# Routed attention with a bilinear FFN on one core: when the softmax denominators are summed, and how the last key tile reaches the sum

## The chip, the core and the metric

The kernel runs on one core of a Trainium2 chip. The core has a matrix engine (TensorE, PE; its weight loads are PEld), a vector engine (VectorE, DVE), an activation engine (ScalarE, ACT), a general one (GpSimd, POOL) and one that only issues transfers (SyncE, SP). Each engine works through its own list of instructions in order, and semaphores make one engine wait for another. The kernel fixes all these lists itself, when it is built. The metric is the device time of one execution in microseconds, the median of several.

## What is computed

The reference, cut to what matters:

```python
# q, k, v: (4 batch, 8 heads, 768 tokens, 64); 16 cluster centroids per head
q_assign = argmax(normalized q @ normalized centroids)     # same for k
mask = q_assign[..., :, None] == k_assign[..., None, :]
scores = where(mask, q @ k.T / sqrt(64), -1e9)
attn = exp(scores - max(scores))
attn = attn / (attn.sum(-1) + 1e-9)
x = (attn @ v) as a (3072 tokens, 512) matrix
out = ((x @ w_a) * (x @ w_b)) @ w_out                      # w_a, w_b: 512 x 1536, w_out: 1536 x 512
```

Everything is float32. A row of attention is divided by its denominator, the sum of its exponentials over all 768 keys.

## The kernel before

The heads are taken in pairs, 16 in all: pair p belongs to batch element p // 4. For each pair the queries are cut into two halves of 384 tokens, and the keys into six tiles of 128. A unit u is one pair, one half and one key tile; it has 12 units per pair. The main loop takes two units per pass, called a group g; three groups make a half, six make a pair, and 96 groups make the attention. What stands in a group:

```python
for g in range(NG + 3):                  # NG = 96
    p, l = divmod(g, GPP)                # pair, and group within it (GPP = 6)
    now, before = (2*g, 2*g + 1), (2*g - 2, 2*g - 1)
    ...
    if 0 < g < NG:  score(now)           # TensorE: mask and q.k; ACT: exponentials pt
    check_inverses()
    if 0 < g <= NG:
        for u in before: add_up(u)       # sums of pt over the key tiles
    if 1 < g <= NG: weigh(before)        # TensorE: pt times v into O
    late = int(g > EARLY)
    if g % 3 == late and 0 < g - late:
        denominators(*divmod(g // 3 - 1, 2))
    if g < NG: ready[l]()                # prepares the next pair: transposes, clusters, one-hot
    ...                                  # due[g]: which weight parts are rounded in this group
    round_next()
    first, second = (4, 1) if g <= EARLY else (5, 3 if g < NG else 2)
    ph = {first: (p, 0), second: (p - 1, 1)}.get(l)
    halved = ph in den_of
    if halved: todo.extend(normalize(*ph))
    if ffn:                              # pieces of the FFN fill the rest of the group
        credit += PER_GROUP[...]
        while len(ffn) > least and credit > 0:
            cost, piece = ffn.popleft(); credit -= cost
            piece()
            if todo: todo.popleft()()
            round_next()
    else: credit = 0
    round_next()
    while todo: todo.popleft()()
    if halved: ffn_ready(*ph)            # FFN pieces of a batch element, once its x is whole
```

While the first batch element's attention runs (pairs 0 to 3, groups 0 to 23) there is no FFN to fill the groups; the FFN of a batch element runs beside the attention of the next.

The exponentials of one half are summed over the six key tiles (j from 0 to 5) in a tile acc of 128 x 768. In the first batch element (p < HP, HP = 4) VectorE adds; later the sum is made by accumulating transfers that POOL issues. Matmuls with ones then sum over the 128 keys of a tile:

```python
def add_up(u):
    p, hf, j = where(u)
    if j == 0 or j == NJ - 1 and p < HP: return
    if j == 1: accs[p, hf] = accp.tile([P, 2, HB], FP32, name="acc")
    acc = accs[p, hf]
    if p < HP:
        nc.vector.tensor_tensor(out=acc, in0=probs[u - 1] if j == 1 else acc, in1=probs[u], op=ALU.add)
        return
    if j == 1: nc.vector.tensor_tensor(out=acc, in0=probs[u - 1], in1=probs[u], op=ALU.add)
    else:      nc.gpsimd.dma_start(out=acc, in_=probs[u], accum_op=ALU.add)

def denominators(p, hf):
    ps = apart()
    acc = accs.pop((p, hf))
    terms = [acc]
    if p < HP: terms.insert(0, probs[p * UPP + hf * NJ + NJ - 1])    # the last key tile
    for n, t in enumerate(terms):
        for a in range(2):
            nc.tensor.matmul(out=ps[a * D:(a + 1) * D, 0:HB], lhsT=ones, rhs=t[:, a, :],
                             start=(n == 0), stop=(n == len(terms) - 1))
    nc.scalar.activation(out=acc[:, 0, :], in_=ps[:, 0:HB], func=AF.Copy, accum_out=...)
```

Normalization of a half takes three steps on VectorE (transpose, reciprocal, transpose back, on acc) and a multiply of x on POOL. Weights are rounded in 36 parts of 128 x 512: four instructions on VectorE and an add on POOL for each, then see_w checks their size with two activations on ACT and starts the next load:

```python
def round_w(i):     # vector: tensor_scalar, scalar_tensor_tensor (w); tensor_scalar, scalar_tensor_tensor (rest)
    ...             # gpsimd: w = w + rest
    unseen.append((i, upper half of raw))

def see_w():
    while unseen:
        i, upper = unseen.pop()
        nc.scalar.activation(out=size, in_=upper, func=AF.Abs)
        nc.scalar.activation(out=size, in_=size, func=AF.Relu, ..., accum_out=stat[:, n:n + 1])
        load_w(i + 2)
```

The up part of the FFN computes 2 x 2 blocks by seven products, p1 to p7, on sums and differences of blocks; T1 to T4 are the combinations of x, made on VectorE. The pieces come in the order p1, p2, p6, p5, p7, p3, p4; p6 reads T2, p7 reads T3. For the first batch element T2 is made when its x is whole, and T3 beside p2:

```python
elif n == 0:                       # first batch element
    ps[1] = both(ps[1], lambda: combine_x(b, "T3"))
    ps[3] = both(lambda: combine_x(b, "T4"), ps[3])
```

Of the kernel before, what the change touches and what calls it, by code (L numbers as in the profile page):

```python
# [8 lines left out]
FP32 = mybir.dt.float32  # L9
BF16 = mybir.dt.bfloat16  # L10
INT32 = mybir.dt.int32
UINT32 = mybir.dt.uint32
# [22 lines left out]
P = 128  # L35
# [107 lines left out]
def short_path(nc, tc, ctx, c, cn, centroids_in, casts, n_far, q, k, v,  # L143
# [126 lines left out]
        raws[i] = raw  # L270

    def round_w(i):
        w = w_parts[i][0]
        wi = w.bitcast(INT32)
        raw = raws.pop(i)
        halves = lambda dt: raw.bitcast(dt).rearrange("p (n two) -> p n two", two=2)
        lo, hi = halves(UINT32)[:, :, 0], halves(INT32)[:, :, 1]


        nc.vector.tensor_scalar(out=wi, in0=hi, scalar1=3, scalar2=0x3FFFFFF8,  # L280
                                op0=ALU.logical_shift_left,
                                op1=ALU.bitwise_and)
        nc.vector.scalar_tensor_tensor(out=wi, in0=hi, scalar=SIGN_TOP, in1=wi,
                                       op0=ALU.bitwise_and, op1=ALU.bitwise_or)

        rest = wtp.tile([P, WN], FP32, name="rest")
        nc.vector.tensor_scalar(out=rest.bitcast(INT32), in0=wi,
                                scalar1=SIGN_EXP, scalar2=None,
                                op0=ALU.bitwise_and)
        nc.vector.scalar_tensor_tensor(out=rest, in0=lo, scalar=2.0 ** -52,  # L290
                                       in1=rest, op0=ALU.mult, op1=ALU.mult)
        nc.gpsimd.tensor_tensor(out=w, in0=w, in1=rest, op=ALU.add)
        unseen.append((i, halves(FP32)[:, :, 1]))

    unseen = []

    def see_w():

        while unseen:
            i, upper = unseen.pop()
            size = spare()[0].bitcast(BF16)[:, 3 * WN:4 * WN]
            nc.scalar.activation(out=size, in_=upper, func=AF.Abs)
            n = 4 * NPAIR + i
            nc.scalar.activation(out=size, in_=size, func=AF.Relu, scale=-STEEP,
                                 bias=edge[:, 0:1], accum_out=stat[:, n:n + 1])
            load_w(i + 2)

    NSTAT = 4 * NPAIR + len(w_parts)  # L310
    edge = zero.tile([P, 1], FP32, name="edge")
# [231 lines left out]

    probs, accs, O_of, den_of, xTs = {}, {}, {}, {}, {}
    unchecked = []
    todo = deque()
    UPP = 2 * NJ
    NU = NPAIR * UPP
# [33 lines left out]

    def add_up(u):
        p, hf, j = where(u)
        if j == 0 or j == NJ - 1 and p < HP:
            return
        if j == 1:
            accs[p, hf] = accp.tile([P, 2, HB], FP32, name="acc")
        acc = accs[p, hf]
        if p < HP:  # L590
            nc.vector.tensor_tensor(out=acc, in0=probs[u - 1] if j == 1 else acc,  # L591
                                    in1=probs[u], op=ALU.add)
            return
        if j == 1:
            nc.vector.tensor_tensor(out=acc, in0=probs[u - 1], in1=probs[u],  # L595
                                    op=ALU.add)
        else:
            nc.gpsimd.dma_start(out=acc, in_=probs[u], accum_op=ALU.add)  # L598

    def weigh(us):  # L600
        for u in us:
# [16 lines left out]

    def denominators(p, hf):


        ps = apart()
        acc = accs.pop((p, hf))
        terms = [acc]
        if p < HP:
            terms.insert(0, probs[p * UPP + hf * NJ + NJ - 1])
        for n, t in enumerate(terms):
            for a in range(2):
                nc.tensor.matmul(out=ps[a * D:(a + 1) * D, 0:HB], lhsT=ones,  # L629
                                 rhs=t[:, a, :], start=(n == 0),  # L630
                                 stop=(n == len(terms) - 1))
# [149 lines left out]
    def ffn_ups(b, h):  # L781
# [109 lines left out]
        for n, (combinations, ps) in enumerate(parts):  # L891
            if n == 0 and b:
                ps[0] = both(*combinations, ps[0])
                ps[2] = both(lambda: combine_x(b, "T4"), ps[2])
            elif n == 0:
                ps[1] = both(ps[1], lambda: combine_x(b, "T3"))
                ps[3] = both(lambda: combine_x(b, "T4"), ps[3])
            if n + 1 < len(parts):
                for i, step in enumerate(parts[n + 1][0], 4):
                    ps[i] = both(ps[i], step)  # L900
            pieces += [(2 * HB, f) for f in ps]
# [10 lines left out]
    def ffn_downs(b, h):  # L912
# [96 lines left out]

        def before():  # L1010
            see_w()
            assert not raws
# [17 lines left out]
    def both(*fs):  # L1030
        return lambda: [f() for f in fs]
# [19 lines left out]
    def ffn_ready(p, hf):  # L1051

        b, hp = divmod(p, HP)
        if hp < HP - 1 or hf == 0:
            return
        if b > 0:
            h = []

            ffn.insert(len(ffn) - FREE_ROOM, (0, lambda: (
                up_room(b), combine_x(b, "T3"), combine_x(b, "T1"))))  # L1060
            ffn.insert(len(ffn) - 1, (0, lambda: combine_x(b, "T2")))
            ffn.extend(ffn_ups(b, h)[1])
        else:
            h = h_first
            combine_x(0, "T2")
            ffn.extend(ups_first + plain_ups(0, h, range(NF - 4, NF)))
        ffn.extend(ffn_downs(b, lambda: h))

# [18 lines left out]
    early = early_steps()  # L1087

    for _ in range(12):
        nc.tensor.matmul(out=idle[0:D, 0:D], lhsT=ones, rhs=ones, start=True,  # L1090
# [31 lines left out]
    for g in range(NG + 3):  # L1122
        p, l = divmod(g, GPP)
        if l == 0:
            ready = prep_steps(p + 1)
        now = (2 * g, 2 * g + 1)
        before = (2 * g - 2, 2 * g - 1)
        if g == 1:
            weigh(before)
        if 0 < g < NG:  # L1130
            score(now)
        check_inverses()
        if 0 < g <= NG:
# [9 lines left out]
        parts = due.get(g, [])  # L1143
        if g in early:
            todo.append(early[g])

        def round_next():
            if parts or not ffn:
                see_w()
            if parts:  # L1150
                i = parts.pop(0)
                round_w(i)
# [298 lines left out]
```

## Time and profile before

| what | value |
|---|---|
| time, median of 3 | 1055.83 us (1055.52 to 1056.8) |
| span of the profiled execution | 1052.8 us |
| TensorE busy | 1023.8 us, 97% |
| VectorE busy | 579.2 us, 55% |
| ScalarE busy | 336.5 us, 32% |
| GpSimd busy | 254.1 us, 24% |
| accumulating transfers acc<-pt | 96, of 384 KB each |

The profile is one execution. A line of a timeline has the start and the length in us, the engine, the line of the kernel, the operation, what it writes and reads by the program's names, and in brackets the idle time before it with what ended it. A line of waits has the waiting instruction, what it waited for, the total in us, how often, and the longest. The lines of the kernel that matter: L563 are the scores, L572 the exponentials, L591 and L595 the adds of VectorE into acc, L598 the accumulating transfers, L606 the product with v, L629 the denominators, L649 to L661 the normalization, L692 all FFN matmuls, L779 the combinations of x, L280 to L292 the rounding, L304 and L306 the size check. TensorE splits a float32 matmul in two, so a matmul of the program is two in the trace.

### The profile page before, as it was taken

How to read it: one execution, taken by the hardware profiler on the slowest of the kernel's cores; microseconds unless marked ns; L12 is line 12 of the kernel's file. 1: busy time of each engine (PE TensorE's matmuls, PEld its weight loads, DVE VectorE, ACT ScalarE, POOL GpSimd, SP SyncE). 2: the span in 40 equal slices, each digit the busy share in tenths (PEclk: the TensorE clock that was granted, in tenths of full speed). 3: DMA queues.
4: the chain of work that ended last, by engine and by line, in shares of the span. 5: the costliest groups of instructions: out<-in, count | busy, mean ns of one | idle time of the engine just before them, and what ended most of it. 6: DMA issues, size and time to landing. Idle time of an engine off the chain costs nothing.

```text
span 1052.8 us, 17688 instructions
## 1 busy us (share of the span) xinstructions
PE 1023.8 (97%) x7094; PEld 499.5 (47%) x7094; DVE 579.2 (55%) x1098; ACT 336.5 (32%) x674; POOL 254.1 (24%) x251
## 2 busy tenths in 40 slices
PE   8999989989999999999999999999999999999997
PEld 5443333334445554444444655444444566444564
DVE  6668777786658345443545535444443635444552
ACT  5666544444542213333233121233232201111100
POOL 1112234354332112222324211232222110212100
PEclk9999989999999999999999999999999999999999
DMA  7334546857574463626243372533322320000000
GB/s 181 87 83 88 102 90 147 167 129 154 140 156 86 94 112 65 109 46 106 54 81 65 78 134 54 91 61 66 60 45 50 76 56 21 1 1 1 6 31 29
DMA packets 134346, 84.24 MB, mean 80 GB/s; under 512 B 108144, under 2 KB 117360, under 8 KB 134256
## 3 DMA queue, kind: packets, MB, share of 16 engines
q0 software_dynamic: 13824, 37.75, 19.8%
q1 hardware_dynamic: 120016, 44.85, 19.0%
q8 instruction: 58, 0.95, 0.4%
q10 hardware_dynamic: 416, 0.43, 0.1%
q14 instruction: 32, 0.26, 0.1%
HBM read 37.78 MB, written 6.29 MB: 42 GB/s over the span
## 4 chain that ended last, share of the span: by engine, by line
PE 80%; DMA 6%; DVE 6%; issue 4%; POOL 2%; ACT 2%; DVEq 0%; POOLq 0%; SPq 0%; ACTq 0%
PE m L692 54%; PE s L563 12%; PE O L606 10%; DMA acc<-pt 5%; PE s L629 1%; PE m L629 1%; PE s L378 1%; DVE acc L591 1%; ACT pt L572 1%; PE m L378 1%; POOL xT L661 0%; DVE acc L595 0%; POOL acc L598 0%; POOL h L840 0%; PE m L362 0%
## 5 line engine op out<-in xcount | busy, mean ns | idle before, releaser
L572 ACT ACTIVATE pt<-s 128x768 f32<-128x768 f32 x192 | 146.2, 808 | 191.1 <-PE s L563 142.6
L598 POOL DMA_DIRECT2D acc<-pt x96 | 82.8, 862 | 261.1 <-DMA acc<-pt 161.5
L606 PE MATMUL O<-pt,v 128*64 128x384 f32 x768 | 145.0, 499 | 0.0
L563 PE MATMUL s<-qkT 64*128 64x384 f32 x768 | 140.3, 484 | 0.0
L840 POOL TENSOR_TENSOR h<-h,ha 128x384 f32<-128x384 f32 x66 | 72.8, 1110 | 214.6 <-DVE ha L834 213.7
L834 DVE TENSOR_TENSOR ha<-ha,m 128x384 f32<-128x384 f32 x88 | 48.1, 549 | 126.7 <-PE m L692 100.9
L830 ACT COPY h<-m 128x384 f32<-128x384 f32 x88 | 42.2, 480 | 213.3 <-PE m L692 209.9
L834 DVE TENSOR_TENSOR h<-h,m 128x384 f32<-128x384 f32 x88 | 48.2, 547 | 100.9 <-PE m L692 73.5
L606 PEld LDWEIGHTS O<-pt,v 128*64 128x64 f32 x768 | 46.6, 136 | 85.8 <-issue 77.9
L692 PE MATMUL m<-wo_sb,h 128*64 128x256 f32 x768 | 86.7, 379 | 0.0
L692 PE MATMUL m<-xT,wa_sb 128*64 128x384 f32 x480 | 83.7, 487 | 2.7 <-DVE ha L834 2.5
L563 PEld LDWEIGHTS s<-qkT 64*128 64x128 f32 x768 | 71.0, 188 | 31.8 <-issue 0.9
L692 PE MATMUL m<-xT,wb_sb 128*64 128x384 f32 x480 | 83.1, 486 | 0.4 <-DVE h L834 0.4
L692 PE MATMUL m<-raw 128*64 128x384 f32 x432 | 78.9, 486 | 0.0
L692 PEld LDWEIGHTS m<-wo_sb,h 128*64 128x64 f32 x768 | 56.1, 137 | 29.1 <-issue 3.7
L661 POOL TENSOR_TENSOR xT<-xT,acc 128x384 f32<-128x384 f32 x32 | 35.2, 1099 | 133.4 <-DVE acc L656 84.1
L692 PE MATMUL m<-xT,h 128*64 128x256 f32 x576 | 64.6, 379 | 0.0
L692 PE MATMUL m<-xT,pair 128*64 128x384 f32 x352 | 64.5, 487 | 0.0
L830 ACT COPY ha<-m 128x384 f32<-128x384 f32 x66 | 31.6, 478 | 98.8 <-PE m L692 93.2
L692 PEld LDWEIGHTS m<-xT,wa_sb 128*64 128x64 f32 x480 | 34.9, 137 | 46.1 <-issue 33.2
L692 PEld LDWEIGHTS m<-xT,wb_sb 128*64 128x64 f32 x480 | 34.6, 137 | 43.5 <-issue 37.0
L692 PEld LDWEIGHTS m<-xT,h 128*64 128x64 f32 x576 | 42.1, 137 | 21.4 <-issue 1.6
(180 smaller groups left out, 1323.6 us busy)
## 6 DMA issues: line engine op xcount, KB each, us to landing
acc<-pt POOLq DMA_DIRECT2D x96, 384.0 KB, 4.0
raw<-in_moe_w_a_dram SPq DMA_DIRECT2D x12, 512.0 KB, 4.2
raw<-in_moe_w_b_dram SPq DMA_DIRECT2D x12, 512.0 KB, 3.7
raw<-in_moe_w_out_dram SPq DMA_DIRECT2D x12, 512.0 KB, 3.9
qk<-in_q_dram SPq DMA_DIRECT2D x48, 96.0 KB, 3.3
qk<-in_k_dram SPq DMA_DIRECT2D x48, 96.0 KB, 3.7
v<-in_v_dram SPq DMA_DIRECT2D x24, 192.0 KB, 3.9
out_dram<-rest SPq DMA_DIRECT2D x24, 128.0 KB, 1.7
```

Of the source, the lines that this page charges most:

```text
L378: nc.tensor.matmul(out=ps[32 * kq:32 * kq + 32, 0:HB], lhsT=cTb[:, hp, :], rhs=qkTs[p][:, kq * HB:(kq + 1) * HB], start=True, stop=True)
L563: nc.tensor.matmul(out=s[:, a, 0:HB], lhsT=Ts[p][r, S + j * P:S + (j + 1) * P], rhs=Ts[p][r, hf * HB:(hf + 1) * HB], start=start, stop=not ...
L572: nc.scalar.activation(out=pt, in_=s[:, :, 0:HB], func=AF.Exp, scale=SCALE)
L591: nc.vector.tensor_tensor(out=acc, in0=probs[u - 1] if j == 1 else acc, in1=probs[u], op=ALU.add)
L598: nc.gpsimd.dma_start(out=acc, in_=probs[u], accum_op=ALU.add)
L606: nc.tensor.matmul(out=O_of[0][a * D:(a + 1) * D, 0:HB], lhsT=vs[p][:, a, j, :], rhs=probs[u][:, a, :], start=(j == 0), stop=(j == NJ - 1))
L629: nc.tensor.matmul(out=ps[a * D:(a + 1) * D, 0:HB], lhsT=ones, rhs=t[:, a, :], start=(n == 0), stop=(n == len(terms) - 1))
L661: nc.gpsimd.tensor_tensor(out=x, in0=x, in1=den, op=ALU.mult)
L692: nc.tensor.matmul(out=ps[half], lhsT=lhsT[:, half], rhs=rhs, **kw)
L830: nc.scalar.copy(out=box[name], in_=box["X"][:, 0:HB])
L834: nc.vector.tensor_tensor(out=box[name], in0=box[name], in1=box[bank][:, 0:HB], op=ALU.add)
L840: nc.gpsimd.tensor_tensor(out=to, in0=to, in1=box[name], op=ALU.mult)
```

## The change

The last key tile of the first batch element's halves (j = 5) is no longer a term of its own in the denominators, but is added to acc by an accumulating transfer, so that the denominators have one term everywhere. To leave time for it, the denominators of a half come a group later in the first batch element, and with them the normalization and the start of the FFN. In the later batch elements the transfers of odd key tiles (3 and 5) are issued at the end of their group, so that two in a row don't hold up POOL's list, and the denominators come after two FFN pieces of their group instead of ahead of them. Rounding and the size check of a weight part are cut into two steps each and are spread over the FFN pieces, T3 is made right after T2, and the rates of FFN and rounding are set to the later start.

The diff, cut (marked ...):

```diff
     def round_w(i):
...
+        def first():
+            see_w()
+            ...                          # the two vector instructions that write w
+        def second():
+            ...                          # the two that write rest, and the add on gpsimd
+            unseen.extend(see_steps(i))
+        return [first, second]
+
+    unseen = deque()
+    def see_steps(i):
+        def first():
+            ...
+            nc.scalar.activation(out=size, in_=upper[:, :, 1], func=AF.Abs)
+        def second():
+            nc.scalar.activation(out=size, in_=size, func=AF.Relu, ...)
+            del raws[i]
             load_w(i + 2)
+        return [first, second]
+
+    def see_w(steps=None):
+        for _ in range(len(unseen) if steps is None else min(steps, len(unseen))):
+            unseen.popleft()()
...
     def add_up(u):
         p, hf, j = where(u)
-        if j == 0 or j == NJ - 1 and p < HP:
+        if j == 0:
             return
...
-        if p < HP:
+        if p < HP and j < NJ - 1:
             nc.vector.tensor_tensor(out=acc, in0=probs[u - 1] if j == 1 else acc,
                                     in1=probs[u], op=ALU.add)
             return
...
         else:
-            nc.gpsimd.dma_start(out=acc, in_=probs[u], accum_op=ALU.add)
+            add = lambda: nc.gpsimd.dma_start(out=acc, in_=probs[u],
+                                              accum_op=ALU.add)
+            add() if p < HP or j % 2 == 0 else at_the_end.append(add)
...
         acc = accs.pop((p, hf))
-        terms = [acc]
-        if p < HP:
-            terms.insert(0, probs[p * UPP + hf * NJ + NJ - 1])
-        for n, t in enumerate(terms):
-            for a in range(2):
-                nc.tensor.matmul(out=ps[a * D:(a + 1) * D, 0:HB], lhsT=ones,
-                                 rhs=t[:, a, :], start=(n == 0),
-                                 stop=(n == len(terms) - 1))
+        for a in range(2):
+            nc.tensor.matmul(out=ps[a * D:(a + 1) * D, 0:HB], lhsT=ones,
+                             rhs=acc[:, a, :], start=True, stop=True)
...
             elif n == 0:
-                ps[1] = both(ps[1], lambda: combine_x(b, "T3"))
                 ps[3] = both(lambda: combine_x(b, "T4"), ps[3])
...
             combine_x(0, "T2")
+            combine_x(0, "T3")
...
-        (UP * 11 / 12 + DOWN * 7 / 8, BG + 2.8), ((UP + DOWN) * 7 / 8, BG + 0.8),
+        (UP * 11 / 12 + DOWN * 7 / 8, BG + 1.8), ((UP + DOWN) * 7 / 8, BG + 0.8),
...
-    EARLY = BG + 1
+    EARLY = BG + 2
...
-        due.setdefault(26 + int((i - 8) / 1.5), []).append(i)
+        due.setdefault(27 + int((i - 8) / 1.6), []).append(i)
...
-        late = int(g > EARLY)
-        if g % 3 == late and 0 < g - late:
-            denominators(*divmod(g // 3 - 1, 2))
+        halves = [divmod(g // 3 - 1, 2)] if g % 3 == 1 and g > 1 else []
+        def sums_across():
+            while halves:
+                denominators(*halves.pop())
+        if not ffn:
+            sums_across()
+        pieces = 0
...
-        round_next()
-        if g <= EARLY:
-            first, second = 4, 1
-        else:
-            first, second = 5, 3 if g < NG else 2
+        if not ffn:
+            see_w(1)
+            round_next()
+        first, second = (5, 2) if g <= EARLY else (5, 3 if g < NG else 2)
...
                 piece()
                 if todo:
                     todo.popleft()()
-                round_next()
+                for _ in range(cost // HB // 2):
+                    round_next()
+                pieces += 1
+                if pieces == 2:
+                    sums_across()
         else:
             credit = 0
-        round_next()
+            round_next()
+        sums_across()
         while todo:
             todo.popleft()()
+        while at_the_end:
+            at_the_end.pop(0)()
```

More of the change, by code (lines that the diff above doesn't have):

```diff
@@ L274, in round_w @@
         wi = w.bitcast(INT32)
[L275 to L304, printed above, removed]
+        halves = lambda dt: raws[i].bitcast(dt).rearrange(
+            "p (n two) -> p n two", two=2)
+        def first():
+            see_w()
+            hi = halves(INT32)[:, :, 1]
+            nc.vector.tensor_scalar(out=wi, in0=hi, scalar1=3, scalar2=0x3FFFFFF8,
+                                    op0=ALU.logical_shift_left,
+                                    op1=ALU.bitwise_and)
+            nc.vector.scalar_tensor_tensor(
+                out=wi, in0=hi, scalar=SIGN_TOP, in1=wi, op0=ALU.bitwise_and,
+                op1=ALU.bitwise_or)
@@ new lines, in second @@
+        def second():
+            rest = wtp.tile([P, WN], FP32, name="rest")
+            nc.vector.tensor_scalar(out=rest.bitcast(INT32), in0=wi,
+                                    scalar1=SIGN_EXP, scalar2=None,
+                                    op0=ALU.bitwise_and)
+            nc.vector.scalar_tensor_tensor(
+                out=rest, in0=halves(UINT32)[:, :, 0], scalar=2.0 ** -52, in1=rest,
+                op0=ALU.mult, op1=ALU.mult)
+            nc.gpsimd.tensor_tensor(out=w, in0=w, in1=rest, op=ALU.add)
+            unseen.extend(see_steps(i))
@@ L305, in see_w @@
+        return [first, second]
+    unseen = deque()
+    def see_steps(i):
+        size = spare()[0].bitcast(BF16)[:, 3 * WN:4 * WN]
+        def first():
+            upper = raws[i].bitcast(FP32).rearrange("p (n two) -> p n two", two=2)
+            nc.scalar.activation(out=size, in_=upper[:, :, 1], func=AF.Abs)
+        def second():
             n = 4 * NPAIR + i
@@ L545, in short_path @@
     unchecked = []
+    at_the_end = []
     todo = deque()
@@ L1011, in before @@
             see_w()
-            assert not raws
+            assert not raws and not rounding
             down_room()
@@ L1085, in short_path @@
     for i in range(8, len(w_parts)):
-        due.setdefault(26 + int((i - 8) / 1.5), []).append(i)
+        due.setdefault(27 + int((i - 8) / 1.6), []).append(i)
     early = early_steps()
+    rounding = deque()
     for _ in range(12):
@@ L1137, in short_path @@
             weigh(before)
-        late = int(g > EARLY)
-        if g % 3 == late and 0 < g - late:
-            denominators(*divmod(g // 3 - 1, 2))
+        halves = [divmod(g // 3 - 1, 2)] if g % 3 == 1 and g > 1 else []
[5 more added lines that the diff above has]
+        pieces = 0
         if g < NG:
             ready[l]()
-        parts = due.get(g, [])
+        for i in due.get(g, []):
+            rounding.extend(round_w(i))
         if g in early:
@@ L1147, in round_next @@
         def round_next():
[L1148 to L1152, printed above, removed]
-        round_next()
-        if g <= EARLY:
-            first, second = 4, 1
-        else:
-            first, second = 5, 3 if g < NG else 2
+            if rounding:
+                rounding.popleft()()
+        if not ffn:
+            see_w(1)
+            round_next()
+        first, second = (5, 2) if g <= EARLY else (5, 3 if g < NG else 2)
         ph = {first: (p, 0), second: (p - 1, 1)}.get(l)
```

## The prediction

> **What bounds the kernel now.** I read the page first, then the waits of TensorE, then its busy time in stretches of 20 us, and last the timelines around each wait. The page and the sums by stretch:
>
> ```profile
> span 1052.8 us, 17688 instructions
> PE 1023.8 (97%) x7094; PEld 499.5 (47%) x7094; DVE 579.2 (55%) x1098; ACT 336.5 (32%) x674; POOL 254.1 (24%) x251
> acc<-pt POOLq DMA_DIRECT2D x96, 384.0 KB, 4.0
> ```
>
> TensorE leaves only 29 us of the span unused; by its timeline about 9 of them lie before its first and after its last matmul. Its work is the same whatever the order, so the change can win only what it removes from TensorE's list, or some of about 20 us of holes. These stretches show where the holes are:
>
> ```profile
> 100.00:120.00 20.00, 18.70 (x120) 7.79 (x118) 17.57 (x26) 11.47 (x24) 6.39 (x4) 1.00 0.25 67
> 120.00:140.00 20.00, 14.38 (x84) 5.85 (x82) 14.04 (x26) 6.37 (x12) 6.43 (x7) 0.84 0.82 160
> 220.00:240.00 20.00, 17.68 (x112) 7.58 (x109) 16.95 (x30) 8.82 (x20) 8.75 (x9) 1.00 0.55 126
> 400.00:420.00 20.00, 20.00 (x135) 9.28 (x132) 10.10 (x20) 6.10 (x12) 3.01 (x4) 1.00 0.36 73
> ```
>
> The columns are the length, then busy us of PE, PEld, DVE, ACT and POOL, the granted clock, the DMA share, GB/s. From 300 us on TensorE is full but for 0.4 us near 367 and 1.5 near 854; before that VectorE is busy up to 88% and TensorE has holes. The waits of TensorE over the span name them:
>
> ```profile
> PE m L692 <- DVE h L779: 5.6, 1, 5.6
> PE s L629 <- DMA acc<-pt: 4.9, 4, 1.8
> PE m L692 <- DVE ha L834: 2.5, 2, 2.3
> PE s L563 <- ACT pt L572: 2.0, 6, 0.4
> PE m L629 <- DVE acc L591: 1.3, 1, 1.3
> ```
>
> L629 is the denominators, L779 a combination of x, L692 the FFN. In windows of 2 us the one long hole also costs clock:
>
> ```profile
> 132.00:134.00 2.00, 0.00 (x0) 0.00 (x0) 1.63 (x4) 0.00 (x0) 0.73 (x2) 0.90 0.98 184
> 134.00:136.00 2.00, 0.21 (x2) 0.24 (x4) 2.00 (x2) 0.00 (x0) 1.49 (x2) 0.50 0.72 177
> 138.00:140.00 2.00, 2.00 (x10) 0.99 (x10) 1.34 (x5) 0.48 (x1) 0.20 (x1) 0.50 0.45 82
> ```
>
> **What the Trainium skill says.** "TensorE: Matmul & The Clock Gate", Part 1: an idle window of about 3.4 us drops the array to half clock, and as long a busy one restores it. The trace agrees: after 5.6 us idle the clock reads 0.50 until about 140.4. "DMA: Bandwidth & Descriptors", SWDGE vs HWDGE vs iDMA: an accumulating transfer can be issued by GpSimd alone; its Anatomy section fits 2.0 us plus bytes over 436 GB/s, an estimate of 2.9 us for 384 KB. The trace has more, 4.0 us in the median over the run and 3.9 to 8.3 between 120 and 300 us, and I use the trace. The same page, Rules for kernel authors: a second accumulation on the same bytes must wait for the first one's semaphore; the trace shows that as 161.5 us in which POOL waited for acc<-pt. "SBUF — State Buffer", Who interferes with whom: a VectorE instruction with two SBUF inputs and a GpSimd one that reads SBUF block each other; here an add of 0.95 us takes up to 1.57 beside a POOL multiply.
>
> **The change part by part: gains.**
>
> (a) One-term denominators. In the first batch element each of the 8 halves had one more term, four matmuls in the trace (m<-pt,ones, 32 in all) that pass in 0.65 us (eight, both terms, take 1.29 in the chain of waits). 8 x 0.65 = 5.2 us, all on TensorE's path.
>
> (b) The waits of the old denominators for VectorE's add: 1.3 us near 105, and 0.15 in each of three more halves, seen between the two lines at 53.44 and 54.40 below. Together 1.7 us.
>
> (c) The size check on weights (two ACT instructions of 0.66 and 0.72 us plus a 0.19 read) stood between the two one-hot copies, and the next exponentials came late; TensorE lost 0.66 us in each of three pairs. The change splits it and lets it run a group later, behind the exponentials. 2.0 us.
>
> (d) Start of the FFN. The 5.6 us hole is L779, the combination T3: TensorE reached it while VectorE stood behind weight rounding, which stood behind POOL, which stood behind an accumulating transfer. The change computes T3 right after T2, before the first piece, and starts a group later, so that it has two bare groups (3.16 us each: L563 1.72, L606 1.44) to be ready. I take all 5.6, and the clock: 4.6 us at half rate after the restart (135.8 to 140.4) cost 2.3 more. 7.9 us.
>
> (e) After the start, about 9.2 us of small holes remain up to 855: 4.9 at denominators behind transfers, 4.3 at FFN pieces behind ACT and VectorE, which are busy with rounding. The denominators move behind two pieces (2.6 us in the up part, 5.2 in the down part), the odd transfers to the group's end, and rounding goes in smaller portions. But the last transfer then also starts later: issued up to 1.3 us before the group's end and landing 4.5 to 6 after that, against 3.16 + 2.6 = 5.7 until the denominators. In the down part this fits (8.3 us), in the up part it is close. I take half, 4.7 us.
>
> Gains: 5.2 + 1.7 + 2.0 + 7.9 + 4.7 = 21.5 us.
>
> **The cost.** The last key tile of a half now comes by a transfer that can start only after the add before it, and the denominators stand one group later. A bare group is 3.16 us, and the transfer alone takes 4.0. So I followed VectorE's, POOL's and TensorE's lists around the old denominators near 54 us:
>
> ```profile
> 50.48 0.56 DVE L425 TENSOR_REDUCE mx<-m 128x24 f32<-128x384 f32 x1 [3.21 <-PE m L392]
> 53.39 0.95 DVE L591 TENSOR_TENSOR acc<-acc,pt 128x768 f32<-128x768 f32 x1
> 53.44 0.81 PE L629 MATMUL m<-pt,ones 128*64 128x384 f32 x4
> 54.40 0.87 PE L629 MATMUL m<-acc,ones 128*64 128x384 f32 x4
> 57.38 0.57 DVE L649 STREAM_TRANSPOSE acc<-acc 128x384 f32<-128x384 f32 x1
> 57.99 0.23 DVE L652 RECIPROCAL inv<-acc 128x12 f32<-128x12 f32 x1
> 58.25 0.58 DVE L656 STREAM_TRANSPOSE acc<-inv 128x384 f32<-128x384 f32 x1
> 58.97 1.56 POOL L661 TENSOR_TENSOR xT<-xT,acc 128x384 f32<-128x384 f32 x1 [0.15 <-DVE acc L656]
> ```
>
> VectorE starts five cluster-assignment steps at 50.48, when TensorE's transposes are through, and the add follows at 53.39. The normalization of the half before ran earlier in the old order. In the new build's instruction order its three VectorE steps (1.37 us, 57.38 to 58.75) stand between the assignment and this add, and its multiply on POOL (1.0 to 1.56) stands before the transfer. So: 53.4 + 1.4 = 54.8 normalized; the POOL multiply to about 56.2; the add to 55.7, beside it; the transfer from 56.2 to 60.2. TensorE would reach the denominators at 53.44 + 3.16 = 56.6. It waits 3.6 us. That is pair 1, and pair 2 is the same. In pair 0 there is no half before: the add ends at 28.0, the transfer starts 0.5 later and lands at 32.5, TensorE comes at 27.1 + 3.2 = 30.3, and waits 2.3. In pair 3 the assignment goes by 32-row blocks and POOL has a one-hot step of 2.0 us; with normalization moved behind it I get POOL's one-hot from 102.7 to 104.7, its multiply to 106, landing near 110.4, against TensorE at 104.1 + 3.2 = 107.3: 3.1 us. The second half of each pair has transposes in between and an add that starts early: in pair 1 the transfer lands near 68.1, and TensorE comes at about 71. No wait.
>
> Cost: 2.3 + 3.6 + 3.6 + 3.1 = 12.6 us. The weight load that falls into the same group may add 0.3 each, and a wait of 3.6 us can cover a whole clock window, though seldom; for both I add 1.4, which makes 14.
>
> The sum is 21.5 - 14 = 7.5 us off, and 1055.8 - 7.5 gives 1048.3 us, 0.7% faster.
>
> **Rivals.** First: the transfer hides after all, because VectorE has more slack than I read, or transfers land in under 4 us. For it speaks that the second halves have 2.9 us to spare; against it, that 3.16 is less than 4.0 before any work on VectorE is counted, so pair 0 waits in any case. If it held, the whole 21.5 us would come: 1034 us. Second: the new waits grow. Eight more transfers of 384 KB share the DMA engines with weight and q/k loads (0.82 busy from 120 to 140), and transfers there took up to 8.3 us; in the FFN's up part the last transfer now starts at the group's end, where the next q/k load starts too. If eight such halves wait 1 us each and half-clock stretches follow the four waits of the first stage (four times about 2 us), the gain is gone: 1048 + 16 = 1064. Third: TensorE's holes at the FFN's start only move. The transfers there stand in POOL's list before the one-hot step and the first rounding add, one after the other, some 13 us for three. If VectorE again stands behind them, 3 to 5 us of (d) stay: 1053. The idea that all of it hides in any case has little behind it: TensorE is the bound in every stage, and each hole in its list is time.
>
> **Range and chances.** (a) is nearly sure, (b) and (c) likely, (d) likely in most of its size, (e) open by 4 us either way, and the cost open by about 5. Taken together I expect 1048.5 us, with 1040 to 1057 as the range for 8 in 10. Faster by over 2% means under 1034.7, which needs every gain and no new wait: 0.05. Slower by over 2% means over 1077: 0.02. Within 2%: 0.93.
>
> **What would show it.** Right: m<-pt,ones gone and TensorE's denominators of the first batch element waiting for DMA acc<-pt, four waits of 2 to 4 us, in the first halves of pairs 0 to 3 only; no wait for a combination at the FFN's start and a clock of 1.00 between 120 and 140; no waits for pt before L563. (c) is wrong if these stay. (e) is right if waits of L692 and of the denominators after 140 us add up to 4 to 5 us. The prediction is wrong if the four waits are absent, or longer than 5 us with a clock of 0.50 behind them, or if the eight second halves in the FFN's up part wait as well.

## The result, and the profile after

The changed kernel takes 1110.31 us (median of 4 runs, 1109.68 to 1113.52) against 1055.67 for the kernel before: a ratio of 1.053, with a 95% interval of 1.0497 to 1.0563. It is slower by 5.3%, where 0.7% faster was predicted. First the page of the changed kernel, the same three lines as before:

```profile
span 1108.6 us, 17659 instructions
PE 1036.3 (93%) x7062; PEld 503.1 (45%) x7062; DVE 571.8 (52%) x1098; ACT 336.2 (30%) x674; POOL 261.4 (24%) x259
acc<-pt POOLq DMA_DIRECT2D x104, 384.0 KB, 4.0
```

TensorE has 32 matmuls fewer, as meant, yet is busy 12.5 us longer, which with fewer instructions means a lower clock: 0.981 of full speed was granted over the span, 0.995 before. The unused part of the span grew from 29 to 72 us. The waits of TensorE name what it waits for. L647 is now the denominators, L709 the FFN, L847 ScalarE's copies of FFN results, L593 the exponentials, L584 the scores; `s` and `m` are the buffers written:

```profile
PE s L647 <- DMA acc<-pt: 25.7, 17, 3.5
PE m L709 <- ACT h L847: 17.1, 6, 5.3
PE m L647 <- DMA acc<-pt: 13.6, 5, 3.7
```

The third line is the cost that was predicted: denominators of the first batch element, before the FFN has begun (they write m). The first two lines were not: 43 us, in the denominators of the later batch elements (they write s) and in the FFN. One of the stretches shown of before, where TensorE was busy for 17.68 us at full clock, now reads (columns as before):

```profile
220.00:240.00 20.00, 16.65 (x86) 7.11 (x88) 13.73 (x26) 8.82 (x20) 8.67 (x9) 0.83 0.42 98
```

A sum over the timelines nearly closes the account. TensorE's idle time between its first and its last matmul adds up to 64.6 us (20.5 before), which is 44.1 more; 37.5 us ran at half clock (6.8 before), which costs at most half of the difference, 15.4; 32 matmuls less give 5.2 back. That is 54.3, and TensorE's last matmul ends 56.5 us later (1101.9 against 1045.4). By place: the last product with v of group 24 (the end of the first batch element's scores) ends at 126.25 instead of 116.61 us, 9.6 later, and the other 46.9 us are lost after it. So most of the loss lies behind the first batch element's scores, where steps (d) and (e) of the prediction change the order.

Three timelines show the mechanisms. The first is pair 1 of the first batch element, the place that the prediction worked out from before's timeline:

```profile
55.28 1.58 POOL L678 TENSOR_TENSOR xT<-xT,acc 128x384 f32<-128x384 f32 x1 [10.08 <-ACT pair L319]
56.80 0.87 POOL L619 DMA_DIRECT2D acc<-pt  x1
...
60.77 1.55 PE L647 MATMUL m<-acc,ones 128*64 128x384 f32 x4 [3.69 <-DMA acc<-pt]
```

VectorE's list is as predicted: the assignment to 53.78, the normalization, the add from 55.07 to 55.99, with the multiply of the normalization ahead of the transfer on POOL. The transfer starts at 56.80 and TensorE goes on at 60.77. The wait is 3.69 us; 3.6 had been predicted. But its matmuls take 1.55 us for four, where the same four took 0.87 after the first wait: the clock has fallen to half.

The second timeline is in the FFN's up part:

```profile
208.64 0.50 PE L584 MATMUL s<-ohT 64*128 64x384 bf16 x4
...
213.70 1.28 POOL L300 TENSOR_TENSOR wb_sb<-wb_sb,rest 128x512 f32<-128x512 f32 x1 [3.08 <-DVE rest L297]
214.91 0.93 POOL L619 DMA_DIRECT2D acc<-pt  x1
...
219.38 0.81 ACT L593 ACTIVATE pt<-s 128x768 f32<-128x768 f32 x1 [8.03 <-DMA acc<-pt]
...
221.00 2.83 PE L709 MATMUL m<-h,wa_sb 128*64 128x384 f32 x8 [5.26 <-ACT h L847]
```

The transfer at 214.91 is that of key tile 3 of half 10 (halves counted from 0 over the whole kernel), held back to its group's end. That end comes late in POOL's list: TensorE had left the group and begun the next one's scores at 208.64, but POOL still had two rounding adds to do before the transfer, and the second waited 3.08 us for VectorE. The transfer's source is one of four pt buffers, and the exponential four later (key tile 1 of half 11) writes that buffer. ScalarE therefore stands for 8.03 us until the landing. It works in order, so the copy of an FFN result behind it comes at 220.45, and TensorE, whose last matmul before it ended at 215.7, stands for 5.26 us. Over the whole kernel the exponentials' waits for transfers, before and after, are

```profile
ACT pt L572 <- DMA acc<-pt: 13.4, 7, 3.0
...
ACT pt L593 <- DMA acc<-pt: 116.8, 29, 8.0
```

The third shows how the denominators come to wait, in half 18:

```profile
491.91 0.50 PE L584 MATMUL s<-ohT 64*128 64x384 bf16 x4
...
492.00 2.31 POOL L857 TENSOR_TENSOR h<-h,ha 128x384 f32<-128x384 f32 x2 [2.26 <-DVE ha L851]
494.27 0.99 POOL L678 TENSOR_TENSOR xT<-xT,acc 128x384 f32<-128x384 f32 x1
495.22 0.87 POOL L619 DMA_DIRECT2D acc<-pt  x1
...
499.30 0.87 PE L647 MATMUL s<-acc,ones 128*64 128x384 f32 x4 [1.58 <-DMA acc<-pt]
```

TensorE begins the next group at 491.91. The transfer of key tile 5, held to the end of the group before, stands in POOL's list behind two FFN products (L857), which waited for VectorE, and behind the multiply of the normalization. It starts at 495.22, when TensorE is 3.3 us into the next group. TensorE comes to the denominators at 497.72, 5.8 us into the group (the prediction had 5.7), and waits 1.58 us. So it goes in general: in the 23 later halves that another group's scores follow, the last transfer starts 0.3 to 6.2 us after those scores have begun, 2.8 us in the median.

The last half shows a second way, in POOL's list:

```profile
900.06 0.86 POOL L619 DMA_DIRECT2D acc<-pt  x1
904.50 0.87 POOL L619 DMA_DIRECT2D acc<-pt  x1 [3.58 <-DMA acc<-pt]
909.01 0.86 POOL L619 DMA_DIRECT2D acc<-pt  x1 [3.64 <-DMA acc<-pt]
```

Each addition must wait until the one before it has landed, so the three (key tiles 3, 4 and 5) follow each other 4.4 to 4.5 us apart. The one that was held back pushes the next two back; TensorE comes to the denominators at 909.58 and waits 3.52 us. Of the 17 waits only this one and that of half 12 are of this kind. In the other 15 the transfer of key tile 4 had landed 2.3 to 20.1 us before that of tile 5 was issued, and POOL's own work ran right up to the issue.

### The profile page after: what moved, and what is told of

It reads as the page before. It is cut to its first block, busy times and chain, and to the rows that moved or that the text cites. A ratio compares the mean times of both kernels' runs of the same rounds, so it can differ in the third digit from the quotient of the medians.

```text
span 1108.6 us, 17659 instructions
## 1 busy us (share of the span) xinstructions
PE 1036.3 (93%) x7062; PEld 503.1 (45%) x7062; DVE 571.8 (52%) x1098; ACT 336.2 (30%) x674; POOL 261.4 (24%) x259
## 3 DMA queue, kind: packets, MB, share of 16 engines
q0 software_dynamic: 14976, 40.90, 20.5%
## 5 line engine op out<-in xcount | busy, mean ns | idle before, releaser
L593 ACT ACTIVATE pt<-s 128x768 f32<-128x768 f32 x192 | 150.4, 810 | 309.0 <-PE s L584 127.4
L584 PE MATMUL s<-qkT 64*128 64x384 f32 x768 | 142.4, 490 | 0.0
L857 POOL TENSOR_TENSOR h<-h,ha 128x384 f32<-128x384 f32 x66 | 72.2, 1100 | 268.0 <-DVE ha L851 267.4
L619 POOL DMA_DIRECT2D acc<-pt x104 | 90.1, 868 | 160.1 <-DMA acc<-pt 117.8
L851 DVE TENSOR_TENSOR ha<-ha,m 128x384 f32<-128x384 f32 x88 | 48.5, 551 | 149.2 <-PE m L709 103.1
L847 ACT COPY h<-m 128x384 f32<-128x384 f32 x88 | 42.2, 480 | 167.8 <-PE m L709 164.4
L709 PE MATMUL m<-wo_sb,h 128*64 128x256 f32 x768 | 86.9, 379 | 0.0
L584 PEld LDWEIGHTS s<-qkT 64*128 64x128 f32 x768 | 72.3, 191 | 32.2 <-issue 2.1
L709 PE MATMUL m<-xT,wb_sb 128*64 128x384 f32 x480 | 86.1, 499 | 0.0
L709 PE MATMUL m<-xT,wa_sb 128*64 128x384 f32 x480 | 83.7, 487 | 0.0
L709 PE MATMUL m<-raw 128*64 128x384 f32 x432 | 79.2, 487 | 2.3 <-ACT ha L847 1.6
L709 PEld LDWEIGHTS m<-wo_sb,h 128*64 128x64 f32 x768 | 55.9, 137 | 29.5 <-issue 3.7
L709 PE MATMUL m<-xT,pair 128*64 128x384 f32 x352 | 64.6, 488 | 0.0
L709 PE MATMUL m<-xT,h 128*64 128x256 f32 x576 | 64.6, 379 | 0.0
L847 ACT COPY ha<-m 128x384 f32<-128x384 f32 x66 | 31.7, 480 | 93.3 <-PE m L709 87.6
L709 PEld LDWEIGHTS m<-xT,wb_sb 128*64 128x64 f32 x480 | 35.5, 141 | 45.3 <-issue 39.5
L709 PEld LDWEIGHTS m<-xT,wa_sb 128*64 128x64 f32 x480 | 35.5, 137 | 41.8 <-issue 33.1
L709 PEld LDWEIGHTS m<-xT,h 128*64 128x64 f32 x576 | 41.7, 137 | 21.8 <-issue 2.0
```

The source lines that it names most:

```text
L584: nc.tensor.matmul(out=s[:, a, 0:HB], lhsT=Ts[p][r, S + j * P:S + (j + 1) * P], rhs=Ts[p][r, hf * HB:(hf + 1) * HB], start=start, stop=not ...
L593: nc.scalar.activation(out=pt, in_=s[:, :, 0:HB], func=AF.Exp, scale=SCALE)
L619: add = lambda: nc.gpsimd.dma_start(out=acc, in_=probs[u], accum_op=ALU.add)
L709: nc.tensor.matmul(out=ps[half], lhsT=lhsT[:, half], rhs=rhs, **kw)
L847: nc.scalar.copy(out=box[name], in_=box["X"][:, 0:HB])
L851: nc.vector.tensor_tensor(out=box[name], in0=box[name], in1=box[bank][:, 0:HB], op=ALU.add)
```

## Experiments

The theories. One: holding the odd transfers back is the loss, through both channels just seen, the late landing at the denominators (25.7 us) and the held pt buffer (17.1 us of FFN waits). Two: the loss belongs to the rest of the change, the waits of the first batch element with the half clock behind them and the re-spread FFN, and most of it stays without the hold. The ratios are to the kernel before, from runs on the same chip.

**The change without the hold (a_nodefer).**

```diff
-            add() if p < HP or j % 2 == 0 else at_the_end.append(add)
+            add()
```

> The changed kernel with the deferral undone: odd key tiles' transfers are issued at once again, all else stays. Theory 1 (the deferral is the main loss: late transfers hold up the denominators and keep the pt buffers that the exponentials need, and ACT then holds up the FFN): TensorE's idle time after group 26 falls from 46 us to about 9, its half clock there goes, about 1065 us. Theory 2 (rounding and size checks spread over the FFN pieces make VectorE, POOL and ACT late, the deferral only adds a little): the holes of groups 26 to 37 (19 us idle, 17 us at half clock) stay, about 1085 to 1095 us.

Measured: 1060.73 us, ratio 1.0059 [1.0038, 1.0079]. Of the 54.6 us about 50 are gone. TensorE's waits:

```profile
PE m L647 <- DMA acc<-pt: 13.5, 5, 3.7
...
PE s L647 <- DMA acc<-pt: 1.1, 1, 1.1
```

The 25.7 us became 1.1: in 21 of the 23 halves the last transfer now starts ahead of the next group's scores. The FFN's 17.1 us behind copies of h became 5.8, and the exponentials' 116.8 us for transfers 48.5. The cost in the first batch element stays whole. Theory two falls.

**The hold alone, in the kernel before (b_defer).**

```diff
+            add = lambda: nc.gpsimd.dma_start(out=acc, in_=probs[u], accum_op=ALU.add)
+            add() if j % 2 == 0 else at_the_end.append(add)
...
+        while at_the_end:
+            at_the_end.pop(0)()
```

> The kernel before with the deferral alone: transfers of key tiles 3 and 5 at the end of their group. Theory 1: 1090 to 1105 us, with TensorE waiting for DMA acc<-pt at the denominators and ACT waiting for DMA acc<-pt for 100 us or so in sum. Theory 2: at most 10 us over the kernel before, 1065.

Measured: 1188.18 us, ratio 1.1275 [1.1247, 1.1303], far worse than expected. Here the denominators still stand ahead of the FFN pieces:

```profile
PE s L632 <- DMA acc<-pt: 91.9, 24, 6.4
```

All 24 later halves wait, 3.8 us in the mean, and most of the waits (17) have a stretch at half clock beginning in them or just behind, which the expectation had left out. The same hold costs 133 us here and about 50 in the change, where the denominators stand behind two pieces: that they hide the difference is argued, not shown by itself.

**The first batch element's last tile added by VectorE (a_vec).** The hold stays.

```diff
-        if p < HP and j < NJ - 1:
+        if p < HP:
```

> The changed kernel, but VectorE adds the last key tile in the first batch element (no accumulating transfer there); the denominators keep their one term and their place a group later. If the transfer's latency is what TensorE waits for in the first 126 us, the four waits of 2.7 to 3.7 us and the two stretches at half clock go and the time falls by about 17 us, to 1093. Rival: VectorE, with 8 more adds of 0.9 us, ends them as late as the transfer landed; then waits of 1 to 3 us stay and it is 1100 or more.

Measured: 1100.86 us, ratio 1.0447 [1.041, 1.0485]. The first part came as expected: the waits for a transfer are gone, 2.8 us for VectorE take their place, no half clock comes before group 24, which ends at 113.6 us instead of 126.25. But only about 9 of these 12.6 us reach the end; a new hole of 3.8 us opens at 127 us (the next run explains it). The size was missed by 8 us. The time is the one that the rival named, but not for its reason: VectorE's adds end late by 2.8 us in all, where the transfers had cost 13.6.

**Both edits (a_nodefer_vec).**

> The changed kernel with the deferral undone and VectorE adding the last key tile. If both losses are separate and add up (45 and 17 us), about 1047 us, under the kernel before. If spread rounding is a loss of its own (theory 2), 1065 or more.

Measured: 1047.72 us, ratio 0.9928 [0.9905, 0.995], as expected. Two holes in the FFN's start remain, 3.80 us at 127 and 3.34 at 162. At 127 ScalarE's exponential stands 5.11 us for a transfer's landing, and the copy for the FFN behind it: bare groups take 3.16 us, while transfers follow each other in over 4.

**A fifth pt buffer, the hold kept (a_vec_pt5).** Room for it was made by laying two constants into scratch space and computing a third again where it is used.

```diff
-    ptp = pool("ptp", 4)
+    ptp = pool("ptp", 5)
```

> The changed kernel with VectorE adding the last key tile in the first batch element and with five pt buffers instead of four (room is made by laying two constant matrices and the early one-hot tile into scratch that is free then); the deferral stays. Theory hold: a deferred transfer keeps its pt buffer, the second exponential of a group waits for its landing, and the FFN's copies wait behind it on ACT. Then ACT's waits for DMA acc<-pt fall from 112 us to under 40, TensorE's 18.7 us behind ACT h go with the half clock after them, and it is about 1076 us against 1100.9 for four buffers; the 25 us of waits at the denominators stay. Rival: the late landing at the denominators is all that costs, and a held buffer harms nothing; then 1092 or more.

Measured: 1082.16 us, ratio 1.0264 [1.0237, 1.0291]: 1.8% better than a_vec. This separates the two channels. TensorE's waits for transfers:

```profile
PE s L647 <- DMA acc<-pt: 36.0, 16, 6.4
```

And those of ScalarE:

```profile
ACT pt L593 <- DMA acc<-pt: 12.3, 5, 3.7
```

In a_vec the same two were

```profile
PE s L647 <- DMA acc<-pt: 25.5, 17, 3.6
...
ACT pt L593 <- DMA acc<-pt: 111.6, 27, 8.1
```

The exponentials' waits for transfers fell from 111.6 us to 12.3, and FFN waits for ScalarE's copies of h from 18.7 to none. The held buffer is shown as their cause. The denominators now wait 36.0 us instead of 25.5, which is why the gain was smaller than expected: with the buffer free TensorE runs further ahead of POOL (in half 10 the last transfer starts 8.2 us into TensorE's next group, where it was 4.4 in the change).

**A fifth buffer without the hold (a_nodefer_vec_pt5).**

> As the run without deferral and with VectorE's add of the last tile (1047.7 us), with five pt buffers. If the two holes that are left at the FFN's start (3.8 us near 127 and 3.3 near 162, TensorE behind ACT h, ACT behind DMA acc<-pt) come from held buffers, they go: 1040 to 1042 us. If they come from POOL's and VectorE's rounding, they stay: 1046 to 1048.

Measured: 1043.45 us, ratio 0.9892 [0.9872, 0.9913], a little above the 1040 to 1042 expected. The holes at 127 and 162 are gone and 0.5 us of waits for transfers is left at the exponentials. The fifth buffer is worth 19 us with the hold and about 4 without.

**Held back only by two pieces (a_vec_pt5_mid).** As a_vec_pt5, but the held transfers are issued after two FFN pieces of the group.

```diff
                 if pieces == 2:
                     sums_across()
+                    while at_the_end:
+                        at_the_end.pop(0)()
```

> As the run with VectorE's add of the last tile, five pt buffers and deferral (1082.2 us), but the deferred transfers are issued after two FFN pieces of their group instead of at its end, about 3.9 us earlier in the up part. If the late issue is what makes TensorE wait at the denominators (36 us there), those waits fall under 8 us and the time comes to 1044 to 1050. If it is the order of POOL's list as such (an odd transfer behind any FFN work), half or more of the waits stay: 1060 to 1075.

Measured: 1045.01 us, ratio 0.9923 [0.9904, 0.9943]. The same reordering in POOL's list, issued earlier, costs about 0.3% against no hold at all (ratio 0.9892), and the two intervals overlap:

```profile
PE s L647 <- DMA acc<-pt: 9.4, 4, 2.8
```

36.0 us became 9.4. With the hold to the group's end the last transfer started after the next group's first scores in 23 of 23 halves (3.0 us in the median); now it starts ahead of them in 17 of 23. So the loss at the denominators comes from issuing late, and not from the place of the odd transfers behind other work as such.

**Normalization ahead of the assignment (a_norm_first).** On top of a_nodefer, in the groups up to the FFN's start.

```diff
-            todo.extend(normalize(*ph))
+            (todo.extendleft if g <= EARLY else todo.extend)(
+                normalize(*ph)[::-1 if g <= EARLY else 1])
```

> The changed kernel without deferral (1060.7 us), with the normalization of a half placed ahead of the cluster assignment in VectorE's list up to group 26; the last key tile still comes by a transfer. If the chain of the prediction holds (assignment, normalization, add, POOL multiply, transfer), pairs 1 and 2 wait 2.3 us as pair 0 does instead of 3.7, no wait covers a clock window, and it is about 1053 us. If the transfer's latency alone sets the wait, the order on VectorE changes nothing: 1060.

Measured: 1055.57 us, ratio 1.0012 [0.9998, 1.0025]. The waits of pairs 1 and 2 fell from 3.7 to 2.10 and 2.11 us, which shows that the normalization in VectorE's and POOL's lists made them longer, by 1.6 us, where its VectorE steps take 1.4. The expectation on the clock fell: half clock came all the same, after the wait of 2.11 us though not after that of 2.10. The last section takes that up.

**T3 early, alone, in the kernel before (b_t3).**

```diff
-                ps[1] = both(ps[1], lambda: combine_x(b, "T3"))
...
             combine_x(0, "T2")
+            combine_x(0, "T3")
```

> The kernel before with one part of the change alone: T3 made right after T2. If the 5.6 us hole and its half clock are due to T3's place, about 1048 us. If the hole only moves, to the next piece that needs VectorE behind rounding, 1053 to 1056.

Measured: 1049.02 us, ratio 0.9956 [0.9937, 0.9974]. The hole of 5.6 us and the half clock behind it are gone. Step (d) was right, with about 5 us of its 7.9: waits of 1.3 and 1.6 us remain at 136 and 140 us, and a stretch of 3.4 us at half clock came new at 213.

**The parts that looked good, in the kernel before (b_parts).** T3 early, denominators of one term a group later with the last tile added by VectorE, and the later FFN start with its rates; not the spread rounding and size check, and the denominators still ahead of the pieces.

> The kernel before with three parts of the change and no others: T3 early, denominators of one term a group later in the first batch element (with VectorE adding the last tile instead of a transfer), and the start and rates of the FFN set to that. No deferral, no spread rounding, denominators at their old place in the later groups, four buffers. Sum of the stages measured so far: 121.5 us to group 26 as in the run with VectorE's add, 914.6 from there to the last matmul as in the run with T3 alone, 7.5 behind it: 1043.6 span, about 1045 us. If spreading the rounding and moving the denominators behind two pieces was a gain (part e of the prediction), it is slower than the changed kernel without deferral and with VectorE's add, 1047.7.

Measured: 1058.8 us, ratio 1.0052 [1.004, 1.0064]; the expectation of 1045 was missed, and its other branch came (slower than 1047.7, if (e) holds a gain). TensorE waits 6.02 us for VectorE at 203 us, 4.11 for a transfer at 852. Against a_nodefer_vec (1047.72), which has the spread rounding and size check and the moved denominators besides, it loses 11 us (13 by the ratios). These parts of the change, (c) and the rest of (e), are a gain, not a cost; which of them gives how much wasn't taken apart.

**The same with normalization first and five buffers (b_parts_norm_pt5).**

> The run with the three parts, with five pt buffers and with the normalization ahead of the cluster assignment up to group 26. The waits of 0.65, 0.65 and 1.5 to 2 us at first-stage denominators should go (3 us with their clock), and what exponentials still wait for buffers: 1038 to 1042 us. If VectorE is the bound of the first stage, the first 26 groups stay at 121 us and it is 1043 to 1045.

Measured: 1057.52 us, ratio 1.003 [1.002, 1.0041]; 1038 to 1042 had been expected. The first batch element is clean (group 24 ends at 112.5 us), but a hole of 9.8 us opens at 130. VectorE's timeline at the hole:

```profile
137.96 0.43 DVE L287 TENSOR_SCALAR rest<-wb_sb 128x512 int32<-128x512 int32 x1 [7.19 <-POOL wa_sb L292]
```

The step has stood 7.19 us for POOL's rounding add (L292). That add began at 136.35, behind a transfer that POOL could issue only at 135.79, after 6.11 us of waiting for the one before to land. Rounding in one go thus puts VectorE behind POOL, and POOL behind a transfer: the chain that had made the 5.6 us hole before. In a_best, with the spread rounding and the moved denominators, no such hole is left; that the spread rounding is what breaks the chain is argued from this timeline.

**All that held up, together (a_best).** The changed kernel without the hold, with the last tile on VectorE, five buffers and normalization first.

> The changed kernel without deferral, with VectorE's add of the last tile, five pt buffers, and the normalization ahead of the cluster assignment up to group 26. Against the run without that last step (1043.5 us) the first stage's three waits at the denominators, 0.65, 0.65 and 2.0 us, and the half clock after the third go: about 1039 us. If the normalization then stands in the way of the assignment and VectorE is late at the FFN's start instead, 1043 to 1046.

Measured: 1039.51 us (1038.78 to 1040.73), ratio 0.9869 [0.9852, 0.9885], as expected. It is faster than both kernels, and its page shows little left:

```profile
PE 1015.5 (98%) x7062; PEld 493.7 (48%) x7062; DVE 590.6 (57%) x1105; ACT 334.7 (32%) x674; POOL 256.5 (25%) x251
```

The span is 1037.2 us. TensorE's longest wait for another engine or a transfer is 2.2 us, at an FFN piece behind VectorE.

## Why the prediction was wrong

**(a), (b), (c)** were right. 32 matmuls are gone; no denominators of the first batch element wait for VectorE; no scores wait for pt (1.6 us for ScalarE's copy of the denominators came new).

**(d)** was right in kind. The 5.6 us hole and its half clock are gone, both in the change and in b_t3. The size was about 5 us instead of 7.9. In the change a hole of 2.7 us at 140 us came in its place, behind a copy by ScalarE.

**The cost in the first batch element** was right in place and size for the waits: predicted 2.3, 3.6, 3.6 and 3.1 us, measured 2.74, 3.69, 3.68 and 3.07, and 0.43 in a fifth place. Too small was the term for the clock and the weight load, 1.4 us: two of the waits were each followed by 6.8 us of half clock, at most 5.9 us of loss in all (half of the 11.7 us that TensorE worked in them). One reading of before's trace was low without touching the sum: beside a POOL multiply VectorE's add takes up to 1.76 us (at 425.8), not 1.57.

**The failed step is (e).** It said of the last transfer: "issued up to 1.3 us before the group's end and landing 4.5 to 6 after that, against 3.16 + 2.6 = 5.7 until the denominators. In the down part this fits (8.3 us), in the up part it is close. I take half, 4.7 us." In place of the gain stands a loss of about 50 us (a_nodefer against the change). TensorE's way to the denominators was right (5.8 us in half 18), and a landing took 3.9 to 6.3 us. Wrong was the start: the end of a group in TensorE's list was taken for its end in POOL's. There the held transfer stands behind rounding adds, FFN products and the multiply of the normalization, which wait for VectorE, and it starts 0.3 to 6.2 us after TensorE has gone on, instead of up to 1.3 before. That made 17 waits in the 24 later halves, in the down part too (1.74 us at 375, in a group where TensorE needed 8.4 us to the denominators). Two more things were missing. A transfer held back at tile 3 delays those of tiles 4 and 5, which must each wait for the landing before; this made 2 of the 17 waits. And the estimate followed the transfer only to its reader, the denominators, and not to the next writer of its source: with four pt buffers a held transfer stops the exponential four tiles on, and with it all FFN copies in ScalarE's list. a_vec_pt5 shows this second channel by taking it away, and a_vec_pt5_mid shows that the waits at the denominators come from the late start. By the sign that the prediction set for (e), waits of the FFN and the denominators of 4 to 5 us after 140 us, it failed as well: the two largest groups of them alone are 42.8 us. The rest of (e), smaller rounding steps and denominators behind two pieces, was a gain as argued: with (c) about 11 us, by b_parts against a_nodefer_vec, where 4.7 + 2.0 had been taken.

The second rival named the right place ("in the FFN's up part the last transfer now starts at the group's end"), but gave it eight waits of 1 us and a time of 1064; there were 17, of 1.5 us in the mean. It, too, stopped at the denominators.

What stays open: 2.2 us or more of the account at the top (the term for the clock is an upper bound), and how the 11 us split.

## What to carry to other kernels

The end of a loop pass lies at another time in each engine's list: work put there starts when its own engine comes to it (here up to 6.2 us after TensorE had left). A transfer that is issued later holds its source longer and delays each transfer that must follow it: before holding one back, follow both its reader and the next writer of its source buffer, and count the buffers against delay plus landing (here four buffers, and 4 us of landing). An in-order engine turns a wait for one buffer into a wait for all the work behind it, so a loss can show up at a line that the change doesn't touch. Smaller portions of the slow engines' long steps, together with denominators that come later, paid about 11 us here; the reordering of transfers cost about 50.

## What the runs showed of the hardware

The half clock comes by windows, and not by the length of a wait. The Trainium skill ("TensorE: Matmul & The Clock Gate", Part 1) has free-running windows of 3413 ns, of which an idle one drops the clock and a busy one restores it. The traces agree on the grid: every stretch at half clock that ends before the kernel does is one or more times 3.41 us long, and a grid of 3413.3 ns laid through each trace's clock changes meets all of them within 3 ns. What counts as idle is not an empty window. Over the 14 traces, of the windows at full clock that held 2.05 us or more without a matmul, 55 of 55 were followed by half clock; of those with 1.2 to 1.97 us, none of 70; the six between (1.98 to 2.03) went both ways. At half clock, 0.75 us or more idle kept it down in 25 of 25, and with under 0.6 it came back in 57 of 57. Idle is here what the profile does not count as busy PE. Two waits in the changed kernel show it, in windows laid on the grid:

```profile
28.89:32.31 3.42, 1.46 (x10) 0.43 (x8) 2.92 (x5) 0.24 (x1) 1.76 (x2) 1.00 0.63 115
...
56.20:59.61 3.41, 0.88 (x6) 0.14 (x2) 2.62 (x5) 0.69 (x1) 1.47 (x2) 1.00 0.46 86
59.61:63.03 3.42, 2.27 (x12) 1.08 (x13) 2.63 (x3) 1.58 (x5) 1.91 (x1) 0.50 0.17 30
```

The wait of 2.74 us falls across a border: PE is busy 1.46 us of the first window, 1.96 idle, and nothing follows. That of 3.69 us leaves 0.88 busy in its window, 2.53 idle, and the next one runs at 0.50; there the rest of the wait, 1.15 us, keeps the clock down for one more. So a wait of just over 2 us costs up to 1.7 us more (an estimate, half of 3.41) if it lies within a window, and none if a border cuts it into parts that are short enough. This also explains the waits of 2.10 and 2.11 us in a_norm_first: the one left 2.02 us idle in its window, the other 2.11.
